# Chunked attention and mixture of experts: the first block's order from the list schedule

## The chip, the cores and the metric

The kernel runs on one NeuronCore of a Trainium2 chip. Five engines with queues of their own take part: TensorE (PE, its weight loads PEld), VectorE (DVE), ScalarE (ACT), GpSimd (POOL) and SyncE (SP), which issues the DMAs. The metric is the device time of one execution in microseconds; less is better.

## The reference

Attention in chunks of 32 queries, each chunk over 8 memory rows and a window of 16 + 32 + 8 keys, for 4 batches of 8 heads, 768 positions and 64 values a head. Its result, as 3072 tokens of 512 values, goes through 4 experts whose outputs are weighted and summed.

```python
def _attn_ref(q, k, v, mem_k, mem_v):
    for c in range(nc):                       # chunk 32, left 16, right 8
        k_full = np.concatenate([mem_k, k_ctx], axis=2)
        v_full = np.concatenate([mem_v, v_ctx], axis=2)
        scores = scale * np.matmul(q_c, k_full.transpose(0, 1, 3, 2))
        scores = scores - np.max(scores, axis=-1, keepdims=True)
        a = np.exp(scores)
        a = a / (np.sum(a, axis=-1, keepdims=True) + 1e-09)
        out[:, :, c_start:c_end] = np.matmul(a, v_full)

def _moe_ref(x, domain_probs, w1, w2):
    p = domain_probs / (domain_probs.sum(-1, keepdims=True) + 1e-09)
    for e in range(E):
        h = np.maximum(x @ w1[e], 0.0)
        out += p[:, e:e + 1] * (h @ w2[e])
```

## The kernel before

Attention works on units of 96 positions (three chunks) with all heads; there are 8 units a batch (u = 0 to 7) and 32 in all. Per unit: one load of queries and keys (`qk`), scores on TensorE (S, line 455), copies out of PSUM (line 476), maximum, subtraction, exponential, sum and reciprocal (lines 493 to 504), then products with the reciprocal into a banded matrix `band` (line 513), a transpose on TensorE (T, line 526) with copies into `aT` (line 532), and the product with `v` (X, line 540). X is split into a high and a low part, `xa_hi` and `xa_lo` for units 0 to 3, `xb_hi` and `xb_lo` for units 4 to 7 (lines 560, 566); their sum goes to `xr` (line 569).

Every fp32 product of the experts runs as three products of such parts. Weights are split too: a cast to the high part on ScalarE (line 594) and a subtraction for the low part on VectorE or GpSimd (line 598). A half of a batch is 384 tokens. For the first expert of the first batch, `w1` has 8 tiles f; one product for a tile and a half is 12 matmuls of up to 384 columns (line 640), followed by ReLU parts (lines 651, 652). The second product is 24 matmuls of 512 columns for each 128 tokens (line 684). Later batches use a scheme of seven products instead of eight (`Pair`, `Full`, `Halves`; lines 1112 and 1336).

The program has three parts. The first block covers all eight units of batch 0, the first product of half 0 and the second product of its 384 tokens. Its order on all engines is written out by hand in `FIRST_BLOCK`: Q and V are loads, r weight loads, h and lv, lp weight splits, W and w warm-up matmuls on zeros, S to xl the attention steps, M and N the first product on columns 0 to 191 and the rest (`HALVES` = 6: six of the eight tiles are cut so), g and G the halves of the second product. The second and third parts are plans: operations are added in TensorE's order with their engine, an estimated time, what they read and write, and a due time; `run` tries 60 list schedules with shifted due times and other engines, replays each against noise, keeps the best and emits the instructions in the order of its start times. TensorE's order in a plan is that in which the operations were added. The second part begins with the first product of half 1 (line 1047, `plain_first`), eight tiles f, and the third works on n from 5 to 15, with weights read back through a ring of nine tiles (`ring`). Every plan begins with all engines free at time 0 and all inputs there.

DMAs are in the plans as one queue on SP: an issue takes 0.1 us, the bytes pass at 330 GB/s, and nothing lands before 2.6 us:

```python
if op.engine == "SP":
    dma = max(dma, start + 0.3) + op.bytes / 330e3
    op.end = max(dma, start + 2.0) + 0.6
    free["SP"] = start + 0.1
```

Of the kernel before, what the change touches and what calls it, by code (L numbers as in the profile page):

```python
# [11 lines left out]
F32 = mybir.dt.float32  # L12
# [39 lines left out]
xl2 T3 m2 ev3 M5 m4 X3 m5 xh3 xl3 sh4 N0 p5 n0 h8 lp8 e4 N1 N2 h12 sh5 n1 h9 lp9 n2 e5 t4 h10 lv10 N3 n3 lv12  # L52
h11 N5 lp11 N4 n4 b4 n5 N6 h13 t5 b5 h14 N7 lp13 lv14 n6 h15 T4 ev4 n7 X4 xh4 T5 xl4 R0 lp15 ev5
V6 S6 S7 X5 xh5 p6 xl5 V7 sh6 g0 e6 p7 t6 b6 G0 sh7 e7 t7 b7 g1 T6 ev6 G1 T7 ev7 g2 X6 xh6 xl6 G2 X7 xh7 xl7
"""
HALVES = 6
# [4 lines left out]
SLACK = 25.0  # L61
ENGINES = ("PE", "ACT", "DVE", "POOL", "SP")

TURNS = 60
# [19 lines left out]
class Tile:  # L84


    def __init__(self, make, parts):
        self.make, self.parts, self._ap, self.ops = make, parts, None, []
        self.held = False

    @property
    def ap(self):
        if self._ap is None:
            self._ap = self.make()
        return self._ap


class Op:
    __slots__ = ("engine", "time", "fn", "deps", "succ", "birth", "due", "late", "ways", "early", "left", "ready", "start", "end",
                 "two", "bytes", "index")  # L100

    def __init__(self, engine, time, fn, birth, two, bytes_, index):
        self.engine, self.time, self.fn, self.birth, self.two, self.bytes = engine, time, fn, birth, two, bytes_
        self.deps, self.succ, self.index, self.ways = set(), [], index, None
        self.start = self.end = None


class Plan:
# [6 lines left out]
    def __init__(self):  # L115
        self.ops, self.writers, self.readers, self.tags, self.pe = [], {}, {}, {}, 0.0

    def tile(self, make, tag, bufs, parts=1):
        t = Tile(make, parts)
        places = self.tags.setdefault(tag, [])  # L120
        t.behind = None
# [6 lines left out]
    def have(self, ap, tag=None, parts=1):  # L128
        t = Tile(None, parts)
        t._ap, t.behind = ap, None  # L130
        if tag:
            self.tags.setdefault(tag, []).append(t)
        return t
# [9 lines left out]
    def add(self, engine, time, fn, reads=(), writes=(), two=False, bytes_=0, other=None):  # L143

        op = Op(engine, time, fn, self.pe, two, bytes_, len(self.ops))
        if other:
# [4 lines left out]
        for key in reads + writes:  # L151
            t = key[0] if isinstance(key, tuple) else key
# [17 lines left out]
    def run(self):  # L170

        ops = self.ops
# [6 lines left out]
        for op in ops:  # L179
            op.early = max([d.early + self.took(d) + self.wait(d, op) for d in op.deps], default=0.0)  # L180
            if op.engine == "PE":
# [1377 lines left out]
```

## Time and profile before

| | us |
|---|---|
| median of 3 runs | 1077.26 |
| lowest, highest | 1076.61, 1078.2 |
| the profiled execution | 1078.29 |
| its span, first to last instruction | 1076.5 |
| TensorE busy in the span | 1057.2 (98%) |
| VectorE, ScalarE, GpSimd busy | 754.2, 650.3, 339.2 |
| mean granted clock of TensorE | 0.992 |
| DMA, mean | 266 GB/s |

All stretches below are in microseconds from the start of the span. Busy times are those of one profiled execution. A granted clock of 1.00 is 2.4 GHz, 0.50 is 1.2 GHz. An idle time is put down to what released the instruction behind it.

### The profile page before, as it was taken

What the parts mean: (1) busy time and instruction counts of PE and PEld (TensorE: products, weight loads), DVE (VectorE), ACT (ScalarE), POOL (GpSimd) and SP (SyncE); (2) the same over time, 40 slices, a digit from 0 to 9 for tenths busy, and PEclk for the clock granted to TensorE, in tenths of its full rate; (3) what the DMA queues carried; (4) which work ended last, traced back from release to release, by engine and by line L of the source; (5) the groups of instructions that cost most, each with busy time, mean ns of one, the idle gap of its engine ahead of it and who ended that gap; (6) DMA issues with size and microseconds to landing.
All of it is one profiled execution on the core that took longest, in us unless ns stands there. A gap on an engine that the chain in (4) does not pass through costs nothing.

```text
span 1076.5 us, 20355 instructions
## 1 busy us (share of the span) xinstructions
PE 1057.2 (98%) x7412; PEld 1008.3 (94%) x7412; DVE 754.2 (70%) x1345; ACT 650.3 (60%) x1652; POOL 339.2 (32%) x326
## 2 busy tenths in 40 slices
PE   7989999999999999999999999999999999999998
PEld 6878898988989899999999999999999999999998
DVE  6866786857976347768798875857679564748474
ACT  6546885747855567585765866657593644435261
POOL 3523533636252124243242511215023211303030
PEclk8999999999999999999999999999999999999999
DMA  6535696977978579999998978878777977878783
GB/s 222 205 122 213 242 372 219 357 266 262 388 249 327 195 245 300 310 339 321 344 333 298 310 264 273 260 240 257 249 240 235 314 245 236 268 235 253 246 263 137
DMA packets 169364, 286.61 MB, mean 266 GB/s; under 512 B 14128, under 2 KB 108336, under 8 KB 169264
## 3 DMA queue, kind: packets, MB, share of 16 engines
q1 hardware_dynamic: 169264, 285.31, 77.9%
q8 instruction: 59, 0.97, 0.4%
q14 instruction: 41, 0.34, 0.1%
HBM read 216.06 MB, written 69.21 MB: 265 GB/s over the span
## 4 chain that ended last, share of the span: by engine, by line
PE 91%; DVE 5%; DMA 2%; ACT 1%; issue 1%; SPq 0%; DVEq 0%; ACTq 0%
PE a_ps L1112 23%; PE a_ps L1336 17%; PE moe_ps L1112 17%; PE moe_ps L1092 13%; PE moe_ps L1336 13%; PE s_ps L815 2%; DVE band L513 2%; PE x_ps L833 2%; PE moe_ps L1047 2%; PE moe_ps L640 1%; PE moe_ps L684 1%; DMA t<-s_t 1%; DMA ring<-t 1%; DMA qk_pair<-in_qk_dram 1%; PE x_ps L540 0%
## 5 line engine op out<-in xcount | busy, mean ns | idle before, releaser
L1092 PE MATMUL moe_ps<-w,h_hi 128*128 128x512 f32 x432 | 134.3, 392 | 0.0
L776 DVE TENSOR_TENSOR u<-moe_ps,u 128x384 f32<-128x384 f32 x120 | 66.5, 554 | 76.7 <-PE moe_ps L1112 55.5
L777 POOL TENSOR_TENSOR u<-u,u 128x384 f32<-128x384 f32 x38 | 48.6, 1278 | 179.9 <-DVE us L776 179.6
L765 ACT ACTIVATE u<-u 128x384 f32<-128x384 f32 x132 | 68.7, 524 | 57.8 <-DVE u L776 57.3
L763 ACT COPY u<-a_ps 128x384 f32<-128x384 f32 x120 | 57.1, 476 | 74.0 <-PE a_ps L1112 71.1
L1092 PEld LDWEIGHTS moe_ps<-w,h_hi 128*128 128x128 f32 x432 | 80.3, 188 | 16.9
L1092 PE MATMUL moe_ps<-w,h_lo 128*128 128x512 f32 x216 | 84.4, 391 | 0.0
L1066 DVE SCALAR_TENSOR_TENSOR acc<-a_ps,pr,acc 128x256 f32<-128x256 f32 x116 | 55.6, 480 | 40.0 <-PE a_ps L1336 39.0
L1336 PE MATMUL moe_ps<-ring,A_hi 128*128 128x256 f32 x440 | 81.9, 285 | 0.0
L776 DVE TENSOR_TENSOR A_lo<-u,A_hi 128x384 fp32r<-128x384 f32 x108 | 68.3, 639 | 16.7 <-ACT A_hi L763 16.7
L1066 DVE SCALAR_TENSOR_TENSOR acc<-moe_ps,pr,acc 128x256 f32<-128x256 f32 (+1 forms) x109 | 56.5, 523 | 32.0 <-PE moe_ps L1336 20.0
L887 DVE STREAM_TRANSPOSE aT<-band 32x256 f32<-32x256 f32 x168 | 73.0, 435 | 5.1 <-ACT band L763 2.1
L1112 PE MATMUL a_ps<-xc_hi,ring 128*128 128x384 f32 x352 | 75.5, 336 | 0.0
L1336 PEld LDWEIGHTS moe_ps<-ring,A_hi 128*128 128x128 f32 x440 | 69.9, 194 | 0.0
L1336 PE MATMUL a_ps<-ring,Sa_hi 128*128 128x256 f32 x352 | 65.8, 286 | 2.3 <-DMA ring<-t 2.3
L763 ACT CAST A_hi<-u 128x384 fp32r<-128x384 f32 x132 | 67.1, 512 | 1.0
L869 ACT ACTIVATE s_sb<-s_sb,mx 96x64 f32<-96x64 f32 x192 | 64.4, 337 | 0.7
L777 POOL TENSOR_TENSOR A_lo<-u,A_hi 128x384 fp32r<-128x384 f32 x24 | 25.9, 1083 | 123.4 <-ACT A_hi L763 77.7
L1336 PE MATMUL a_ps<-ring,A_hi 128*128 128x256 f32 x352 | 64.7, 283 | 0.1
L1336 PE MATMUL a_ps<-ring,Sb_hi 128*128 128x256 f32 x352 | 64.8, 283 | 0.0
L1336 PE MATMUL moe_ps<-ring,A_lo 128*128 128x256 f32 x220 | 62.7, 285 | 0.0
L1112 PEld LDWEIGHTS a_ps<-xc_hi,ring 128*128 128x128 f32 x352 | 61.8, 188 | 0.1
(217 smaller groups left out, 3081.7 us busy)
## 6 DMA issues: line engine op xcount, KB each, us to landing
ring<-k SPq DMA_DIRECT2D x132, 512.0 KB, 4.8
ring<-t SPq DMA_DIRECT2D x88, 512.0 KB, 5.5
ring<-w SPq DMA_DIRECT2D x66, 512.0 KB, 5.4
k<-w SPq DMA_DIRECT2D x48, 512.0 KB, 5.2
w<-w SPq DMA_DIRECT2D x40, 512.0 KB, 5.8
raw<-in_w_dram SPq DMA_DIRECT2D x64, 256.0 KB, 5.0
ring<-k SPq DMA_DIRECT2D x44, 256.0 KB, 4.4
qk_t<-in_qk_dram SPq DMA_DIRECT2D x24, 448.0 KB, 5.4
```

The source lines that it names most:

```text
L513: eng.tensor_tensor(out=band[rows, :, at:at + hi - lo], in0=s[rows, :, lo:hi], in1=sm[rows].broadcast_to([CH, H, hi - lo]), op=ALU.mult,)
L763: nc.scalar.copy(out(), x())
L765: nc.scalar.activation(out(), x(), func)
L776: ("DVE", t_dve(cols), lambda: nc.vector.tensor_tensor(out=out(), in0=x(), in1=y(), op=op)),
L777: ("POOL", t_pool(cols), lambda: nc.gpsimd.tensor_tensor(out=out(), in0=x(), in1=y(), op=op)),
L815: nc.tensor.matmul(s_ps.ap[0:UQ, j * NPAIR + g, :], lhsT=qk_t.ap[rows, g * UQ:(g + 1) * UQ], rhs=qk_t.ap[rows, NPAIR * UQ + g * P:NPAIR * ...
L869: now["plan"].add("ACT", t_act(KW) + 0.01, lambda h=h: nc.scalar.activation(s_sb.ap[:, h, :], s_sb.ap[:, h, :], AF.Exp, bias=mx.ap[:, h, : ...
L887: dve(lambda c=c, kb=kb: nc.vector.transpose(out=aT[kb * CH:(kb + 1) * CH, :, c * CH:(c + 1) * CH], in_=band[c * CH:(c + 1) * CH, :, kb * ...
L1066: dve(lambda: nc.vector.scalar_tensor_tensor(out=o.ap[:, cols], in0=ps_ap(), scalar=p_e, in1=o.ap[:, cols], op0=ALU.mult, op1=ALU.add), n_ ...
L1092: nc.tensor.matmul(self.ps.ap, lhsT=h.ap[:, self.rows], rhs=w.ap[:, part, :], start=(i == 0 and k == 0), stop=(i == NF - 1 and k == 2),)
L1112: nc.tensor.matmul(ps.ap[:, 0:SG], lhsT=a()[:, c * P:(c + 1) * P], rhs=y[:, k0 + c, :], start=(first and i == 0), stop=(i == len(steps) - ...
L1336: nc.tensor.matmul(ps.ap[:, cols], lhsT=x.ap[:, rows], rhs=w_ap[:, y, :], start=(begins and k == 0 and i == 0), stop=(k == NP2 - 1 and i = ...
```

## The change

The first block's hand-written order for all engines goes. `FIRST_BLOCK` now names TensorE's operations alone, in an order of its own, and a plan of its own adds all operations of the block and is searched with 600 tries. W is a group of matmuls on zeros (into spare columns of the bank of X). The order of the units on TensorE is T0, T1, T3, T2, T5, T4, T7, T6. Four of the eight tiles are cut in two (`AHEAD`), at 192 columns; the others run on all 384 at once. Units in `STRAIGHT` multiply into the band as before, on VectorE or GpSimd as the plan chooses; the others (0, 3, 5) multiply in place and copy into the band on ScalarE. Copies out of PSUM may go to ScalarE or VectorE. All units from 2 on have score tiles of their own, the 16 weight tiles share eight places, and `xc` lies where these tiles were.

The estimate of a DMA changes in all plans (the first plan keeps 330 GB/s). Each plan takes over from the one before when the engines become free and when its values are there. The plans are tried 100 times instead of 60, and scored by when TensorE is done, the last one by its end.

```diff
+FIRST_TURNS, FIRST_SEED = 600, 1
 FIRST_BLOCK = """
-Q0 r1 r0 r2 Q1 Q2 Q3 r3 r4 Q4 Q5 r5 r7 V0 W40 V1 r6 P0 h0 S0 lv0 h1 p0 S1 lv1 h2 p1 h3 sh0 lv2 S2 sh1 e0 lp3
-p2 S3 e1 p3 t0 S4 b0 T0 h4 t1 b1 lp4 Sa5 ev0 X0 p4 T1 sh2 xh0 ev1 e2 Sb5 X1 xl0 V2 h5 r11 t2 w8 xh1 xl1 h7 b2
-lp5 V3 h6 lp6 Q6 Q7 r9 r8 lp7 r12 r10 r13 r14 V4 r15 sh3 V5 M0 m0 M1 m1 T2 ev2 M2 M3 e3 t3 X2 b3 M4 xh2 m3
...
+W32 S0 S1 S2 W6 S3 W30 T0 W6 X0 T1 W12 X1 S4 W12 M1 T3 M5 X3 M2 T2 S5 X2 S6 M6 N7 N5 N4 N6 N0 N2 T5 N1 N3 S7 X5
+g0 T4 g1 G0 X4 T7 G1 X7 T6 g2 X6 G2
 """
-HALVES = 6
+AHEAD = (0, 2, 2, 0, 0, 2, 2, 0)
+STRAIGHT = (1, 2, 4, 6, 7)
+ASIDE = (6,)
+DMA_ISSUE, DMA_FIRST, DMA_RATE = 0.45, 2.0, 400e3
-TURNS = 60
+TURNS = 100
...
             if e == "SP":
-                dma = max(dma, start + 0.3) + op.bytes / 330e3
-                end[op.index] = max(dma, start + 2.0) + rng.uniform(0.4, 1.4)
-                free[e] = start + 0.1
-        return max(end)
+                dma = max(dma, start + DMA_FIRST) + op.bytes / self.rate
+                end[op.index] = dma + rng.uniform(0.2, 0.9)
+                free[e] = start + DMA_ISSUE
+            op.end = end[op.index]
+        self.done = free
+        return max(end) if self.last else free["PE"]
...
-                dma = max(dma, start + 0.3) + op.bytes / 330e3
-                op.end = max(dma, start + 2.0) + 0.6
-                free["SP"] = start + 0.1
+                dma = max(dma, start + DMA_FIRST) + op.bytes / self.rate
+                op.end = dma + 0.5
+                free["SP"] = start + DMA_ISSUE
...
     def took(self, op):
-        return max(2.6, 2.0 + op.bytes / 330e3) if op.engine == "SP" else op.time
+        return DMA_FIRST + op.bytes / self.rate + 0.5 if op.engine == "SP" else op.time
...
+    def after(self, keys=()):
+        zero = self.done["PE"]
+        free = {e: max(-4.0 if e == "SP" else 0.0, t - zero) for e, t in self.done.items()}
+        ends = {}
+        for key in keys:
+            ends[key] = max([0.0] + [op.end - zero + LATENCY for op in self.writers.get(key, ())])
+        return free, ends
...
-    now = {"plan": Plan()}
+    now = {"plan": Plan({"PE": 0.9, "SP": 0.6, "ACT": 2.0, "DVE": 0.8, "POOL": 4.6}, rate=330e3)}
...
+    spots = fixed(early, "spot", 8)
+    raw_spots = fixed(raw, "raw", 3) + acc_tiles[:3] + spots[:2]
+    s_spots = [t[0:UQ].rearrange("p (h k) -> p h k", h=H) for t in spots[2:]]
+    def zeros(n):
+        def fn():
+            for _ in range(n):
+                nc.tensor.matmul(x_bank[:, DM - P:DM], lhsT=idle, rhs=idle, start=True, stop=True)
+        pe(0.111 * n, fn, [], [])
...
+        if u not in STRAIGHT:
+            dve(lambda: nc.vector.tensor_tensor(
+                out=s.ap, in0=s.ap, in1=sm.ap.broadcast_to([UQ, H, KW]), op=ALU.mult), n_s, [sm], [s], two=True)
...
+                if u in STRAIGHT:
+                    join(dst, src, lambda rows=rows, n=hi - lo: sm.ap[rows].broadcast_to([CH, H, n]), ALU.mult, cols,
+                         [(s, c), sm], [("band", u % 2, c, at)])
+                else:
+                    act(dst, src, cols, [(s, c)], [("band", u % 2, c, at)])
...
+    for word in FIRST_BLOCK.split():
+        now["plan"].word = word
+        do_word(word.rstrip("0123456789"), int(word.lstrip("WSTXMNgG")))
+    with tc.manual_schedule():
+        now["plan"].run(FIRST_TURNS, FIRST_SEED)
...
+    free, ends = before.after(keys)
+    plan = now["plan"] = Plan(free)
```

## Rows read from the trace of the kernel before

**Rows 1.** TensorE's waits from 26.5 us on: engine, line, releaser, total, times, longest

```profile
PE att_ps L526 <- DVE band L513: 3.8, 4, 1.8
PE moe_ps L640 <- ACT xa_hi L560: 0.6, 1, 0.6
PE moe_ps L1047 <- ACT xb_hi L560: 0.6, 1, 0.6
PE x_ps L540 <- ACT aT L532: 0.6, 1, 0.6
...
PE a_ps L1336 <- DMA ring<-t: 2.3, 1, 2.3
```

**Rows 2.** Busy time by stretch, all engines; last granted clock, DMA share, GB/s

```profile
core 0: us, PE busy (x) PEld busy (x) DVE busy (x) ACT busy (x) POOL busy (x), PEclk, DMA share, GB/s
0.00:84.00 84.00, 70.92 (x609) 61.74 (x610) 56.83 (x96) 45.27 (x98) 33.71 (x39) 0.92 0.52 176
...
30.00:60.00 30.00, 27.19 (x273) 25.52 (x274) 26.68 (x49) 16.08 (x40) 16.90 (x14) 1.00 0.58 210
...
500.00:550.00 50.00, 50.00 (x382) 48.86 (x383) 39.29 (x77) 38.13 (x105) 16.46 (x17) 1.00 0.99 338
```

**Rows 3.** TensorE by stretch: length, busy, granted clock, DMA share, GB/s

```profile
13.00:15.00 2.00, 0.28 (x4) 1.00 1.02 360
16.00:26.00 10.00, 8.06 (x64) 0.52 0.50 121
72.00:74.00 2.00, 0.55 (x7) 1.00 0.00 0
74.00:78.00 4.00, 4.00 (x14) 0.57 0.38 115
```

**Rows 4.** TensorE's timeline in the first block: start, duration, line, operation

```profile
1.00 4.45 PE L409 MATMUL moe_ps<-idle 128*128 128x128 bf16 x40 [1.00 <-POOL idle L398]
26.79 1.12 PE L640 MATMUL moe_ps<-xa_hi,w 128*128 128x192 f32 x8
30.39 0.85 PE L526 MATMUL att_ps<-ident,band 96*128 96x96 f32 x8 [0.69 <-DVE band L513]
31.02 1.12 PE L640 MATMUL moe_ps<-xa_hi,w 128*128 128x192 f32 x8
...
68.02 0.83 PE L526 MATMUL att_ps<-ident,band 96*128 96x96 f32 x8
```

**Rows 5.** The chain that ended last, first block: start, duration, what

```profile
40.65 8.30 PE moe_ps L640 x72
56.92 2.07 PE att_ps L455 x32
74.30 4.37 PE moe_ps L684 x12
79.48 2.98 PE moe_ps L684 x12
82.46 0.84 PE x_ps L540 x16
83.85 10.86 PE moe_ps L1047 x60
```

**Rows 6.** Timeline of ScalarE and VectorE, unit 6, and a later unit's band copies

```profile
60.22 1.81 ACT L476 COPY s_sb<-att_ps 32x512 f32<-32x512 f32 x4
62.06 0.68 DVE L493 TENSOR_REDUCE mx<-s_sb 96x8 f32<-96x512 f32 x1 [1.14 <-ACT s_sb L476]
62.78 0.69 DVE L494 TENSOR_TENSOR s_sb<-s_sb,mx 96x512 f32<-96x512 f32 x1
64.29 0.68 DVE L502 TENSOR_REDUCE sm<-s_sb 96x8 f32<-96x512 f32 x1 [0.83 <-ACT s_sb L498]
65.44 2.30 DVE L513 TENSOR_TENSOR band<-s_sb,sm 32x64 f32<-32x64 f32 x3
105.17 1.99 ACT L763 COPY band<-s_sb 32x64 f32<-32x64 f32 x4
```

**Rows 7.** The page's DMA issues: count, size of one, median us to landing

```profile
ring<-t SPq DMA_DIRECT2D x88, 512.0 KB, 5.5
```

More of the change, by code (lines that the diff above doesn't have):

```diff
@@ L126, in tile, with slot, have @@
         return t
-    def have(self, ap, tag=None, parts=1):
+    def slot(self, tag, aps, parts=1):
+        t = self.tile(None, tag, len(aps), parts)
+        t._ap = t.behind._ap if t.behind else aps[len(self.tags[tag]) - 1]
+        return t
+    def have(self, ap, tag=None, parts=1, ends=()):
         t = Tile(None, parts)
-        t._ap, t.behind = ap, None
+        t._ap = ap
         if tag:
             self.tags.setdefault(tag, []).append(t)
+        self.ends.update(((t, i), end) for i, end in enumerate(ends))
         return t
@@ L251, in replay @@
             e = op.engine
-            start = free[e]
+            start = max(free[e], op.floor)
             for d in op.deps:
@@ L398, in tile_chunked_attention_moe @@
     nc.gpsimd.memset(idle, 0.0)
-    spare = {}
-    def warm(n, late=False):
-        if late not in spare:
-            if late:
-                spare[late] = ps_head.tile([P, H, P], F32, name="att_ps")[:, 0, :]
-            else:
-                spare[late] = ps_moe.tile([P, DM], F32, name="moe_ps")[:, 0:P]
-        for _ in range(n):
-            nc.tensor.matmul(spare[late], lhsT=idle, rhs=idle, start=True, stop=True)
     ident = head.tile([P, P], F32, name="ident")
@@ L772, in dve, with moved @@
         now["plan"].add("DVE", t_dve(cols), fn, reads, writes, two)
+    def moved(out, x, cols, reads, writes):
+        now["plan"].add("ACT", t_act(cols, True), lambda: nc.scalar.copy(out(), x()), reads, writes,
+                        other=("DVE", t_dve(cols), lambda: nc.vector.tensor_copy(out=out(), in_=x())))
     def join(out, x, y, op, cols, reads, writes, eng="DVE", psum=False):
@@ L1383, in combine_some, with fixed @@
             make2_combined(*combined.pop(0))
-    plan = now["plan"]
-    w1_of = {}
-    for which, f in made:
-        t = plan.have(None, "w1" if which == 1 else "w2", 4 if which == 1 else 2)
+    def fixed(pool, name, many):
+        return [pool.tile([P, DM], F32, name=name, bufs=many) for _ in range(many)]
+    spots = fixed(early, "spot", 8)
+    acc_tiles = fixed(opool, "acc", 6)
+    raw_spots = fixed(raw, "raw", 3) + acc_tiles[:3] + spots[:2]
+    s_spots = [t[0:UQ].rearrange("p (h k) -> p h k", h=H) for t in spots[2:]]
@@ new lines, in tile_chunked_attention_moe, with early_weights @@
+    x_bank = ps_x.tile([P, DM], F32, name="x_ps")
+    x_out = x_bank[:, 0:NPAIR * UQ].rearrange("p (g q) -> p g q", g=NPAIR)
+    first = {}
+    def zeros(n):
[3 more added lines that the diff above has]
+        pe(0.111 * n, fn, [], [])
+    def early_weights(which, f):
+        r = now["plan"].slot("raw_spot", raw_spots)
+        dma(lambda: r.ap, lambda: (w1 if which == 1 else w2)[0, f], P * DM * 4, [], [r])
@@ new lines, in band_keys, with early_turn, fn @@
+    def band_keys(u):
+        return [("band", u % 2, c, at) for c in range(NCU) for _, _, at in PIECES[c]]
+    def early_turn(u):
+        early_band(u)
+        half = H // 2
+        if u in ASIDE:
+            banks = [bank() for _ in range(2)]
+            a_ps = [lambda t=t: t.ap.rearrange("p (h q) -> p h q", h=half) for t in banks]
+        else:
+            t_ps = new(lambda: ps_head, [P, H, P], "att_ps", 2, parts=2)
+            banks = [(t_ps, i) for i in range(2)]
+            a_ps = [lambda i=i: t_ps.ap[:, i * half:(i + 1) * half, :] for i in range(2)]
+        for i in range(2):
+            def fn(i=i):
+                for h in range(half):
+                    nc.tensor.transpose(a_ps[i]()[:, h, 0:UQ], bands[u % 2][:, i * half + h, :], ident[0:UQ, 0:UQ])
+            pe(0.35, fn, band_keys(u), [banks[i]])
+        for i in range(2):
+            moved(lambda i=i: aTs[u % 2][:, i * half:(i + 1) * half, :], lambda i=i: a_ps[i]()[:, :, 0:UQ],
+                  half * UQ, [banks[i]], [("aT", u % 2, i)])
@@ L1514, in tile_chunked_attention_moe @@
     with tc.manual_schedule():
-        plan.run()
+        plan.run(last=True)
 _INS = ["qk", "v", "probs", "w1", "w2"]
```

468 lines of the change are left out of this document (188 added, 280 removed).

## The prediction

> **What bounds the kernel now.** I read TensorE's waits first, on both sides of 84 us. Behind that point a single wait of any size is left, 2.3 us for a `ring` load in nearly a millisecond; ahead of it stand those for VectorE's `band` products, 3.8 us, and three of 0.6 [rows 1]. The table by stretches says the same: of the first 84 us TensorE is busy for 70.9, so 13.1 us are idle [rows 2]. The whole matter is therefore the first block. Its end is the start of the first matmul of line 1047, at 83.85 us [rows 5], which stood 0.6 us behind `xb_hi` [rows 1].
>
> Idle time isn't all that is lost there. Between 16 and 26 us the granted clock is 0.52, between 74 and 78 it is 0.57: the engine ran mostly at 1.2 GHz instead of 2.4. Ahead of the first drop it had been busy for 0.28 of 2 us (13 to 15), ahead of the second for 0.55 of 2 (72 to 74) [rows 3]. And VectorE is busy for 26.7 of the 30 us from 30 to 60, ScalarE for 16.1 and GpSimd for 16.9 [rows 2]. So the block is a chain per unit, from the scores S over the softmax to the transpose T and the mix X, through a nearly full VectorE; TensorE waits at the T's.
>
> **TensorE's line behind the first M.** Prices at 2.4 GHz: 12 matmuls of 192 columns 1.38 (8.30 for 72), two S 2.07, 12 matmuls of the second product 2.98, X 0.84, 12 matmuls of 384 columns 2.17 (10.86 for 60) [rows 5]; T 0.63, from its start to the next operation's [rows 4]. Before, behind M0 at 26.79 [rows 4]: twelve halves 16.6, two full products 4.3, six T 3.8, six X 5.0, S6 and S7 2.1, 72 matmuls of the second product 17.9. That is 49.7 of the 57.1 us to 83.85. The other 7.4 are 5.6 us of waits (3.8 and three times 0.6 [rows 1]), 1.4 us of low clock (the 12 matmuls from 74.30 took 4.37 instead of 2.98 [rows 5]) and a rest of 0.4.
>
> In the new order only four of the eight products are cut in two (`AHEAD`): eight halves 11.1, four full ones 8.7. With T 3.8, X 5.0, S5 to S7 3.1 and the second product's 17.9, TensorE has 49.6 us of work behind M1. The recut wins 1.1 us, and S5, now behind M1, takes 1.0 back.
>
> **The front, up to M1.** SP now takes up the `qk` loads by their due times, and the three weight loads that stood between the first and the second have late ones; so units 1 to 3 come sooner, which costs nothing. S0 followed the 40 warm-up matmuls, which end at 5.45 [rows 4]; W32 ends at 4.6, and the load had landed by 5.45 at the latest. I take 5.0, so S0 ends at 6.0. A straight unit, unit 6, which had VectorE to itself, took 7.8 us from its first copy out of PSUM (60.22) to its transpose (68.02) [rows 4, 6]. Unit 0 is not straight: it puts one product (as the subtraction, 0.69) and four ScalarE copies (1.99) in the place of three VectorE products in a row (2.30) [rows 6], 0.4 longer: T0 at 14.3.
>
> VectorE then sets T1. Per unit it gives 0.68 (maximum), 0.69, 0.68 (sum), 0.47 up to the band (65.44 less the sum's end) and 2.30 for a straight one, so 4.8; or 0.69 in place of 2.30, so 3.2 [rows 6]. From 7.9 (S0's end, and four copies 1.81) it has units 0 and 1 done at 15.9, and with some 2 us of waiting for the exponentials T1 comes at 17.9.
>
> The warm-up words W are now in TensorE's order and cost time where nothing else holds it: 0.111 us each (4.45 for 40 [rows 4]). W6, S3 and W30 end at about 13.1, under T0's wait. T1 ends at 18.5, W12 at 19.9, partly over the copies that X1 needs. X1 and S4 end at 21.8. The product behind X7 could start 1.39 us behind X7's start [rows 5], so M1 could run at 21.8; the last W12 hides behind nothing and costs 1.3. M1 at 23.1, 3.7 us before M0.
>
> **Stalls behind M1.** Down the line T3 is due at 24.5 and T2 at 28.7. VectorE, free of unit 1 at 17.9, has two `x_lo` (1.0 by estimate, from 0.69 for 512 columns) and unit 3 (3.2), ScalarE the copies (2.0): 24.1. Unit 2, straight, is done at 26.9, but low parts of weights and `h_lo` come in between. Nothing to 3 us are lost here. I take 1.5, since one wait of 0.69 stood ahead of T2 before [rows 4]. The four later T's have their S 11 us or more ahead, and need 1.04 + 7.8; the N products and the second product hide them. Over units 0, 3 and 5 VectorE gets rid of 4.8 us, GpSimd of three products, and ScalarE, the least busy [rows 2], gets 6 more. That PSUM copies may go to VectorE moves work by the planner's choice; ScalarE's four take 1.81 now [rows 6], so it can win up to 0.9 in a chain or lose as much on VectorE, and I count nothing.
>
> Without gaps as those ahead of the two drops I expect no low clock behind M1. The block ends at 23.1 + 49.6 + 0.4 + 1.5 = 74.6; 9.25 us are won.
>
> **The other parts.** The 16 weight tiles now share eight places: a load on SP can stand behind the split of the tile before it, and everything queued on SP behind it stands too, `v` loads among it. Their bound is zero to 1 us; I take zero, since no product of line 640 waited for a weight before, only for `xa_hi` [rows 1]. `xc` lies where the early tiles were and is written by the next plan only; that plan's first eight products (8 x 2.17 = 17 us) use neither `xc` nor new weights, and hide its wait and the first loads. If that cover went, each us would count. The times handed from plan to plan, and 100 tries for 60, rearrange the side engines of 990 us in which TensorE hardly waits: at best the 2.3 us go, at worst waits of that size come. I take 0.
>
> The DMA estimate goes from 0.1 to 0.45 us an issue, for a lone load of 512 KB from 3.6 to 3.8 us in the due times and 2.6 to 3.8 in the schedule (median to landing 5.5 [rows 7]), and from 330 to 400 GB/s. The last one leaves the rows: with 0.99 of DMA time taken, 338 GB/s were moved [rows 2]. Nine loads in a row are 11.8 us at 400 and 14.0 at 338, so the last is expected 2.2 us early. The Trainium skill speaks against the new rate too: "DMA: Bandwidth & Descriptors", section Specifications, gives about 358 GB/s as HBM's limit for one core. By that figure the nine loads take 13.2 us, 1.4 more than planned; the row lies still lower and agrees.
>
> **The sum.** The profiled execution took 1078.29 us, 1.79 more than its span of 1076.5; the median of the runs, 1077.26, lies 0.76 above that span. 1077.26 - 9.25 = 1068.0 us.
>
> **Rivals.** A: VectorE stays the bound. For it speak its 26.7 of 30 us and the tight T3 and T2, against it the 4.8 us that it loses. Then the stretch behind M1 loses its 7.4 us again, the block ends at 23.1 + 49.6 + 7.4 = 80.1, and 3.75 us are won: 1073.5. B: the plan fits. No stall behind M1 (1.5), the last W12 stands in a real wait (1.3), and the wait for the ring load goes (2.3): 1068.0 - 5.1 = 1062.9. For it speaks that the order leaves TensorE no other hole behind M1; against it, that the side engines have some 10% of air at best. C, the other side: ring loads come late. One wait of 2.3 us came in the third plan, which has 11 rounds (n from 5 to 15). If the rate of 400 lets each round's T loads go out that much too late, ten more cost 23 us: 1091. From five on it decides (5 x 2.3 = 11.5 > 9.25). For it speaks the 2.2 us just worked out; against it, that a lone load is now given more time, which pulls issues ahead. D: the change doesn't do what it says. The new search and the handed times lose outside the block what it wins, say four waits of 2.3: 1077.
>
> **How the numbers follow.** Forecast 0.55, A 0.18, B 0.14, C 0.08, D 0.05. From 1061.5 to 1074 the range holds the forecast, nearly all of B, and A; it leaves out C and D. About 0.2%, 2.2 us, is what a measurement of this kernel can tell from no change. Faster by more are the forecast, A and B: 0.87. Same is D: 0.05. Slower is C: 0.08.
>
> **What would show it.** T0 near 14.3, the first M near 23.1, the first matmul of the other half near 74.6; a granted clock of 1.0 from the first M on; no more than some 3 us of TensorE waits behind the block. Rival A shows in waits for `band` of 4 us or more behind M1, C in several waits for `ring`. I am wrong if the block ends behind 80 us or if more than 5 us of waits stand behind it.

## The result and the profile after

The changed kernel takes 1079.21 us (median of 22 runs, 1076.39 to 1083.63), the kernel before beside it 1076.83 (22 runs): a ratio of 1.0021, 95% interval 1.0011 to 1.0031. 1068 was predicted. The profiled execution took 1079.78 us, its span is 1078.0.

The first block came out as worked out. Busy time by stretch of the changed kernel, to be read against [rows 2]:

```profile
core 0: us, PE busy (x) PEld busy (x) DVE busy (x) ACT busy (x) POOL busy (x), PEclk, DMA share, GB/s
0.00:84.00 84.00, 75.81 (x691) 68.01 (x692) 59.24 (x108) 49.05 (x104) 28.90 (x37) 1.00 0.62 213
30.00:60.00 30.00, 29.53 (x248) 27.26 (x247) 27.65 (x54) 20.13 (x44) 10.29 (x10) 1.00 0.59 211
500.00:550.00 50.00, 48.43 (x353) 46.91 (x349) 37.58 (x70) 36.73 (x102) 15.76 (x17) 1.00 0.95 321
```

From 30 to 60 us TensorE is idle for 0.5 us instead of 2.8; VectorE is as full as before (27.65 of 30), and the granted clock is 1.00 throughout. TensorE's timeline has T0 at 15.41, the first product M1 at 23.02 and the first product of the other half, now line 794, at 74.23, where [rows 5] have it at 83.85:

```profile
15.41 0.85 PE L1249 MATMUL att_ps<-ident,band 96*128 96x96 f32 x8 [2.49 <-issue]
...
23.02 1.11 PE L794 MATMUL moe_ps<-xa_hi,w 128*128 128x192 f32 x8
24.98 0.88 PE L1249 MATMUL att_ps<-ident,band 96*128 96x96 f32 x8 [0.35 <-ACT band L503]
...
74.23 1.55 PE L794 MATMUL moe_ps<-xb_hi,w 128*128 128x384 f32 x8
```

So 9.62 us are won by then, and none of them is left at the end. The third row above says where to look: from 500 to 550 us TensorE was never idle before, now it is for 1.6 us. Its waits behind 26.5 us, against [rows 1] (line 860 is the first, line 1084 the second product of the later batches; lines 503 and 521 are the helpers that record ScalarE's copies and VectorE's sums):

```profile
PE a_ps L860 <- ACT u L503: 3.9, 4, 1.4
PE a_ps L860 <- DVE u L521: 3.0, 3, 1.5
PE a_ps L1084 <- DVE A_lo L521: 0.8, 1, 0.8
PE x_ps L1268 <- DVE aT L517: 0.6, 1, 0.6
PE x_ps L1268 <- issue: 0.5, 1, 0.5
PE a_ps L1084 <- DVE acc L814: 0.2, 1, 0.2
```

The wait for `ring` is gone, and 7.9 us of waits for copies and sums have come: 7.1 us for those that free TensorE's banks in PSUM (the copies and sums `u` and `acc`), 0.8 for an operand (`A_lo`).

**The account.** From the first product of line 794 (1047) on, TensorE runs the same 6804 matmuls in the same order in both kernels, so each start can be set against its own start before. Where the difference grows from one matmul to the next by over 0.15 us, I call that an added gap. It counts from start to start, so it is a little longer than the idle time of the same wait (1.59 us for one of 1.43). In these two traces, in us:

| | |
|---|---|
| first block | -9.62 |
| added gaps in the second plan (120 to 396 us of before's time) | +2.56 |
| added gaps in the third plan (396 to 626) | +8.55 |
| waits that only the kernel before has (2.48 at the ring load, 0.34 and 0.26) | -3.07 |
| small differences, under 0.15 us each | +3.13 |
| the last matmul | +1.55 |

In the small ones lies another 1.4 us from 606 to 626: in the kernel before the granted clock fell behind that wait for the ring load, as these windows of its trace show.

```profile
core 0: us, PE busy (x), PEclk, DMA share, GB/s
618.00:620.00 2.00, 0.00 (x0) 1.00 0.96 319
620.00:622.00 2.00, 1.89 (x11) 0.66 1.06 386
622.00:624.00 2.00, 2.00 (x11) 0.50 0.79 274
624.00:626.00 2.00, 2.00 (x19) 0.98 0.37 84
```

Without it the small differences add up to 4.5 us on the other side, spread over the whole run. Two things are to be found, then: who makes the gaps, and what makes the matmuls themselves slower.

### The profile page after: what moved, and what is told of

It is laid out like the page before. It is cut to its first block, busy times and chain, and to the rows that moved or that the text cites. A ratio compares the mean times of both kernels' runs of the same rounds, so it can differ in the third digit from the quotient of the medians.

```text
span 1078.0 us, 20402 instructions
## 1 busy us (share of the span) xinstructions
PE 1057.8 (98%) x7438; PEld 1006.6 (93%) x7438; DVE 747.2 (69%) x1319; ACT 649.1 (60%) x1652; POOL 365.0 (34%) x351
## 4 chain that ended last, share of the span: by engine, by line
PE 83%; DMA 7%; DVE 4%; ACT 3%; POOL 2%; issue 1%; SPq 0%; POOLq 0%; ACTq 0%; DVEq 0%
PE a_ps L860 19%; PE a_ps L1084 16%; PE moe_ps L860 14%; PE moe_ps L840 12%; PE moe_ps L1084 12%; PE moe_ps L794 3%; DMA t<-s_t 2%; PE s_ps L560 2%; DMA t<-t_hi 2%; DMA raw<-in_w_dram 2%; PE x_ps L579 2%; POOL s_t L522 2%; ACT s_sb L615 1%; DVE s_t L521 1%; DMA raw_pair<-in_w_dram 1%
## 5 line engine op out<-in xcount | busy, mean ns | idle before, releaser
L840 PE MATMUL moe_ps<-w,h_hi 128*128 128x512 f32 x480 | 149.6, 393 | 0.0
L840 PEld LDWEIGHTS moe_ps<-w,h_hi 128*128 128x128 f32 x480 | 88.9, 188 | 18.7
L840 PE MATMUL moe_ps<-w,h_lo 128*128 128x512 f32 x240 | 93.8, 391 | 0.0
L521 DVE TENSOR_TENSOR A_lo<-u,A_hi 128x384 fp32r<-128x384 f32 x108 | 74.4, 693 | 19.6 <-ACT A_hi L503 19.4
L522 POOL TENSOR_TENSOR u<-u,u 128x384 f32<-128x384 f32 x33 | 40.1, 1214 | 102.6 <-DVE us L521 98.2
L522 POOL TENSOR_TENSOR u<-u,us 128x384 f32<-128x384 f32 x40 | 46.7, 1168 | 52.9 <-DVE us L521 40.2
```

The costliest lines, as they stand in the source:

```text
L521: ("DVE", t_dve(cols), lambda: nc.vector.tensor_tensor(out=out(), in0=x(), in1=y(), op=op)),
L522: ("POOL", t_pool(cols), lambda: nc.gpsimd.tensor_tensor(out=out(), in0=x(), in1=y(), op=op)),
L840: nc.tensor.matmul(self.ps.ap, lhsT=h.ap[:, self.rows], rhs=w.ap[:, part, :], start=(i == 0 and k == 0), stop=(i == NF - 1 and k == 2),)
```

## The experiments

Theories on the gaps. E: the new estimate of DMAs makes worse second and third plans. G: the other engines and the DMAs can't follow a TensorE that comes earlier, whatever the plan. L: each search is a draw, and this one was unlucky. H, that the handed-over times do it, needs no run: without them the search gives both plans the same order on every engine. On the slower matmuls, P: the place of the tiles.

What all runs gave, ahead of their story. The times are medians, block and gaps come from one profiled execution of each kernel. "330" and "400" are the rate in the estimate of the plan, "old" its form before (0.1 us an issue, nothing before 2.6 us), "new" its form after (0.45 us, 2.0 us ahead of the bytes). Block: start of the other half against before's profiled 83.85. Gaps: added gaps as above, in us.

| kernel | plan 2 | plan 3 | block | gaps, plan 2 | gaps, plan 3 | median | ratio to before |
|---|---|---|---|---|---|---|---|
| before_seed2 | old 330 | old 330 | 0.1 | 0.2 | 1.3 | 1075.07 | 0.9980 |
| before_seed3 | old 330 | old 330 | -1.1 | 0.5 | 1.9 | 1074.93 | 0.9977 |
| before_newdma | new 400 | new 400 | -0.6 | 0.3 | 8.1 | 1083.71 | 1.0056 |
| before_xc_far | old 330 | old 330 | -1.6 | 0 | 0 | 1080.45 | 1.0024 |
| changed kernel | new 400 | new 400 | -9.6 | 2.6 | 8.6 | 1079.21 | 1.0021 |
| seed2 | new 400 | new 400 | -7.9 | 1.1 | 3.8 | 1073.91 | 0.9969 |
| seed3 | new 400 | new 400 | -7.3 | 0.8 | 5.7 | 1076.50 | 0.9993 |
| tries500 | new 400 | new 400 | -7.8 | 0 | 5.6 | 1076.19 | 0.9995 |
| x_near | new 400 | new 400 | -9.6 | 0.6 | 8.4 | 1075.81 | 0.9989 |
| first3 | new 400 | old 400 | -8.4 | 0.7 | 8.6 | 1079.41 | 1.0016 |
| other | old 330 | new 400 | -8.3 | 6.0 | 7.8 | 1083.85 | 1.0075 |
| all_old | old 330 | old 330 | -7.1 | 5.0 | 0.8 | 1079.81 | 1.0021 |
| old_dma | old 330 | old 330 | -9.9 | 4.6 | 0.2 | 1075.48 | 0.9983 |
| old_dma_late | old 330 | old 330 | -7.8 | 3.1 | 0 | 1081.66 | 1.0038 |
| rate23_near | new 330 | new 330 | -7.0 | 7.0 | 1.6 | 1077.57 | 1.0006 |
| mix | new 400 | old 330 | -7.9 | 1.0 | 0 | 1070.55 | 0.9934 |
| rate3 | new 400 | new 330 | -8.3 | 0.6 | 1.6 | 1071.52 | 0.9940 |
| mix_near | new 400 | old 330 | -9.6 | 0.4 | 0.2 | 1068.13 | 0.9909 |
| mix_near_seed2 | new 400 | old 330 | -8.4 | 0 | 1.3 | 1068.27 | 0.9917 |

Several kernels share a plan, operation for operation. The changed kernel's second plan is also that of x_near, first3, mix, rate3 and mix_near, and its gaps there are 0.4 to 2.6 us: on one and the same order they differ by 2 us, and the changed kernel's profile has the most. x_near and other have its third plan too, rate23_near has rate3's. all_old's third plan is that of before; mix, mix_near and old_dma_late have old_dma's.

The wait of 2.3 us for the ring load stands in the profiles of three kernels only, before, before_xc_far and all_old; in the others it is gone, which counts 2.5 us and the low clock behind it for them.

### Undoing the plans' new rules: all_old and old_dma

all_old keeps the new block and gives the second and third plan all their old rules (`self.old` is true for these two plans):

```diff
-TURNS = 100
+TURNS = 60
...
-                dma = max(dma, start + DMA_FIRST) + op.bytes / self.rate
-                end[op.index] = dma + rng.uniform(0.2, 0.9)
-                free[e] = start + DMA_ISSUE
+                if self.old:
+                    dma = max(dma, start + 0.3) + op.bytes / 330e3
+                    end[op.index] = max(dma, start + 2.0) + rng.uniform(0.4, 1.4)
+                    free[e] = start + 0.1
...
-        return max(end) if self.last else free["PE"]
+        return free["PE"] if self.rate == 330e3 else max(end)
...
-    plan = now["plan"] = Plan(free)
+    ends = dict.fromkeys(ends, 0.0)
+    plan = now["plan"] = Plan()
```

> The new first block stays; the two later plans are made by the old rules (DMA estimate of 0.1 us an issue, 330 GB/s, landing from 2.6 us; 60 tries; score by the last end; no times handed over). Theory E (the new DMA estimate makes worse plans behind the block): TensorE's waits behind the block are those of before, some 3 us, and the 9.6 us won in the block stay: about 1067 to 1068 us. Theory G (the side engines or the DMAs can't follow a TensorE that is 9.6 us early, so it is given back whatever the plan): 1076 to 1079, with 8 us or more of waits behind the block. Theory L (each new search is a draw; the one of before was a good one): anything from 1068 to 1079.

old_dma undoes the estimate alone (the second group of these lines, in `schedule` and `took` too) and keeps the tries, the score and the handed times.

> The changed kernel with the old DMA estimate in the two later plans, and nothing else undone (100 tries, new score). Theory E: as with all the old rules, 1067 to 1069 us. If the number of tries or the score is what hurts: 1077 to 1080. Theory G: 1076 to 1079. Theory L: anything from 1068 to 1079.

They took 1079.81 us (ratio 1.0006 to 1.0037) and 1075.48 (0.9966 to 0.9999). Both have next to no gaps in the third plan, and both have 4.6 to 5.0 us in the second, where the changed kernel has 2.6. The gain is given back in either case, but in another place: E as it stood then, 1067 to 1069 us, missed both.

### The estimate alone behind the old block: before_newdma

```diff
...
-                dma = max(dma, start + 0.3) + op.bytes / 330e3
-                op.end = max(dma, start + 2.0) + 0.6
-                free["SP"] = start + 0.1
+                dma = max(dma, start + 2.0) + op.bytes / 400e3
+                op.end = dma + 0.5
+                free["SP"] = start + 0.45
...
```

> The kernel before, hand-written first block and all, with the new DMA estimate in its two plans and nothing else. Theory E: the waits of the changed kernel behind the block come without its block: some 8 to 11 us more than before, 1085 to 1088 us. Theory G: nothing to give back, so 1076 to 1079. Theory L: anything from 1076 to 1088.

1083.71 us, ratio 1.004 to 1.0072, 1.3 us under E's range and clear of G's. The gaps of the third plan are here too, 8.1 us at the same places (the largest at 455 and 482 us), though TensorE comes 9 us later than in the changed kernel. For the third plan that is E, and against G. Its order is close to the changed kernel's (some nine tenths of the operations stand in the same sequence), so the two are hardly two draws.

### Other draws: seed2, seed3, tries500, before_seed2, before_seed3

seed3 and before_seed3 have 3 for 2.

```diff
-    def run(self, turns=TURNS, seed=1, last=False):
+    def run(self, turns=TURNS, seed=2, last=False):
```

> The changed kernel with another seed (2 instead of 1) for the search of the two later plans; the first block is the same. Theory E: the estimate is wrong in every draw, so 1076 to 1081 us. Theory L: a different time, anywhere from 1068 to 1082, with waits in other places. Theory G: 1076 to 1079.

> The changed kernel with seed 3 in the later plans (1 gave 1079.2 us, 2 gave 1073.9). Theory L: a third value between 1068 and 1082. Theory G: 1074 to 1079, since no draw keeps much of the 9.6 us.

```diff
-TURNS = 100
+TURNS = 500
```

> The changed kernel with 500 tries for each later plan instead of 100, seed 1 as in the change. Theory L: a longer search finds a plan with fewer waits behind the block; waits there 3 to 5 us instead of 8, and 1069 to 1074. Theory E (the estimate itself misleads the search): no better than with 100 tries, 1077 to 1081. Theory G: 1076 to 1079.

```diff
-        rng = random.Random(1)
+        rng = random.Random(2)
```

> The kernel before with seed 2 instead of 1 in the searches of its two plans; block, estimate and tries are its own. Theory L (each search is a draw, and the one of before a good one): slower than before by some us, 1079 to 1086, with waits behind the block where before has 3 us. The plans' own scores by their model are 305.5 and 695.1 us for this seed, 306.1 and 691.4 for that of before: from them 3 us slower. Theory G (an early TensorE is held back whatever the plan): nothing is early here, so 1076 to 1078.

> The same with seed 3; its plans score 306.0 and 693.3 us by their own model, 1.8 more than those of before. Theory L: 1077 to 1085, another time than with seed 2. Theory G: 1076 to 1078.

1073.91, 1076.50 and 1076.19 us for the changed kernel, 1075.07 and 1074.93 for the one before. So a draw is worth 2 to 5 us, and the change's was a poor one (L has a share); that before's was a good one, as L had it, is not so, since both others lose the wait for the ring load. But all draws by the new estimate have 3.8 to 8.6 us of gaps in the third plan, and no draw by the old one has over 1.9. Five times as many tries gave 3.0 us, no more than another seed does (2.7 and 5.3), and left 5.6 us of gaps there.

### Splitting the estimate by plan: mix and other

```diff
     def __init__(self, free=None, ends=None, rate=DMA_RATE):
         ...
+        self.old = False
...
     plan = now["plan"] = Plan(*plan.after(
         ...
     ))
+    plan.old = True
```

> The changed kernel with the old estimate of a DMA in the third plan alone; the first and the second plan keep the new one. Theory E, now split by plan: the traces so far give TensorE's added gaps from 445 to 626 us of before's time (third plan) as 0.2 to 2.5 us in the kernels planned by the old estimate and 3.8 to 8.5 us in those planned by the new one, whichever first block stands ahead; in the second plan (120 to 300 us) it is the other way round behind the new block, 4.6 to 5.0 us by the old estimate and 0 to 2.6 us by the new. By E this kernel keeps the better half of each: gaps of at most 2.6 us in the second plan and at most 1.5 us in the third, so about 1069 us (ratio near 0.993). By L (each search is a draw, the estimate means nothing) the gaps add to 5 to 11 us as in the others, 1074 to 1080 us. By G (what follows cannot keep up with an early TensorE) the block's gain is gone by 626 us whatever the estimate: 1075 us or more.

other sets `plan.old` for the second plan instead.

> The changed kernel with the old estimate of a DMA in the second plan alone, the mirror of mix. E by plan: added gaps of TensorE of 4 to 5 us from 120 to 300 us of before's time (all_old 5.0, old_dma 4.6) and of 4 to 8.5 us from 445 to 626 us, so 1079 us (old_dma's 1075.5 plus 4 to 8 us in the third plan) to 1083 us. If the second plan's share was chance, it has under 2.6 us of gaps there and the time is that of the changed kernel or less, 1076 to 1079 us.

1070.55 us (ratio 0.9918 to 0.9949) and 1083.85 (1.0048 to 1.0102): E to 1.6 us in mix, and just beyond the upper end of E in other. The two kernels do the same work and differ by 13 us through its order and place on the side engines alone. It is not that TensorE comes early, either: at 445 us of before's time it is 1.4 us ahead of before in other, which has 7.8 us of gaps in the third plan, 6 us ahead in mix, which has none, and 8.9 ahead in mix_near (below), which has 0.2. That ends G for the third plan. All that TensorE waits for in mix behind 75 us is

```profile
PE a_ps L873 <- ACT u L516: 0.4, 1, 0.4
```

Side by side, the stretch of the third plan in the changed kernel and, 8 us earlier, in mix:

```profile
445.00:485.00 40.00, 36.70 (x238) 34.82 (x237) 29.40 (x49) 28.62 (x74) 17.43 (x17) 1.00 0.98 341
```

```profile
437.00:477.00 40.00, 40.00 (x277) 39.49 (x276) 26.61 (x50) 28.75 (x83) 13.75 (x15) 1.00 0.97 326
```

The DMAs are just as full, and loads of 512 KB take as long (medians for `ring<-k` 6.0 us from 440 to 610 us, and 5.9 from 432 to 602 in mix); TensorE is idle for 3.3 us in the one and never in the other. Nothing is faster in mix, it is only queued otherwise. The gap at 451.54 in the changed kernel shows how. Its timeline, TensorE, ScalarE, VectorE and GpSimd:

```profile
451.54 0.96 PE L860 MATMUL a_ps<-xc_hi,ring 128*128 128x384 f32 x4 [1.43 <-ACT u L503]
```

```profile
450.05 0.52 ACT L505 ACTIVATE u<-u 128x384 f32<-128x384 f32 x1 [2.34 <-DVE u L521]
450.60 0.51 ACT L503 CAST A_hi<-u 128x384 fp32r<-128x384 f32 x1
451.02 0.47 ACT L503 COPY u<-a_ps 128x384 f32<-128x384 f32 x1
```

```profile
444.26 1.21 DVE L521 TENSOR_TENSOR s_t<-s_t,t_hi 128x512 fp32r<-128x512 f32 x1 [1.86 <-POOL s_t L522]
...
447.19 2.23 DVE L633 STREAM_TRANSPOSE aT<-band 32x256 f32<-32x256 f32 x5
449.45 0.56 DVE L521 TENSOR_TENSOR u<-moe_ps,u 128x384 f32<-128x384 f32 x1
```

```profile
441.51 1.09 POOL L522 TENSOR_TENSOR s_t<-raw 128x256 f32<-128x256 f32 x1 [10.12 <-DVE acc L814]
...
444.18 0.74 POOL L522 TENSOR_TENSOR s_t<-raw 128x256 f32<-128x256 f32 x1
```

TensorE waits for a bank. The product that the copy at 451.02 takes out of it was ready by 449.1 at the latest, but the copy stands on ScalarE behind two operations on `u`; these wait 2.34 us for VectorE's sum (449.45), which stands behind 2.2 us of transposes that TensorE needs only at 469 us; and VectorE had lost 1.86 us waiting for GpSimd's part of `s_t`, which GpSimd began after 10.12 us of idle time that, by the trace, a sum of VectorE's ended. The DMAs' part is the same in both kernels: GpSimd's `s_t` sums wait for the store `t<-s_t` to give their buffer free, 18.9 us from 445 to 490 us here and 19.6 in mix's stretch. No DMA ends a wait of TensorE; each link is an in-order queue with something late ahead of something urgent. That the rate makes these gaps is tried below; how it leads the search to such an order is read from this one gap, and not shown further.

### Rate or form: rate3, first3 and rate23_near

```diff
-    ))
+    ), rate=330e3)
```

> The changed kernel with the rate of a DMA in the third plan's estimate at 330 GB/s in place of 400; its form (0.45 us of issue, 2.0 us to the first byte, queueing) stays new. The stretch moved 285 to 341 GB/s at a share of 0.87 to 0.98. If the rate is what misleads the planner, the gaps from 445 to 626 us fall from 8.5 us to under 2.5 us and the time to about 1071 us, as in mix. If it is the form, the gaps stay at 4 to 9 us and the time at 1075 to 1080 us.

first3 is mix with 400e3 for 330e3 in the old form.

> Mix with 400 GB/s in place of 330 in the old estimate of the third plan; its form (0.1 us of issue, nothing on the ring of transfers before 0.3 us, at least 2.0 us to land, 0.4 to 1.4 us of scatter) stays old. If the rate is what misleads the planner, the gaps from 445 to 626 us rise to 4 to 9 us and the time to 1075 to 1079 us; if it is the form, they stay under 2.5 us and the time at mix's 1070 to 1071 us.

1071.52 us (0.9922 to 0.9958) and 1079.41 (1.0002 to 1.0029), with 1.6 and 8.6 us of gaps in the third plan: there it is the rate, and the form has no part that shows. Over all runs that makes six different orders of the third plan at 400 GB/s, with 3.8 to 8.6 us of gaps, and six at 330, with 0 to 1.9. The waits of TensorE in first3 are of the changed kernel's kind again:

```profile
PE a_ps L873 <- ACT u L516: 5.9, 5, 2.1
PE a_ps L873 <- DVE u L534: 1.0, 1, 1.0
```

rate23_near has 330 GB/s in the new form in both plans, and the place of x_near (below).

```diff
-    plan = now["plan"] = Plan(free)
+    plan = now["plan"] = Plan(free, rate=330e3)
```

> Mix_near's place of the tiles, with the new form of the estimate and a rate of 330 GB/s in both the second and the third plan. In the third plan rate3 had 1.3 us of gaps by it, so at most 2.5 us here. In the second plan, if the rate is what counts there too (330 GB/s makes it worse behind the new block), the gaps from 120 to 300 us are 4 to 5 us and the time about 1071 to 1072 us; if the form is (the new form makes it better), they stay under 2.6 us and the time is that of mix_near, 1067 to 1069 us.

1077.57 us (0.9992 to 1.002), 6 us more than the worse of the two expectations for it: 7.0 us of gaps in the second plan, 5.1 of them one wait for a cast of weights on ScalarE, which stood behind GpSimd's sums:

```profile
PE a_ps L861 <- ACT w L504: 5.0, 1, 5.0
```

So the third plan wants 330 GB/s. For the second plan behind the new block the runs point to 400, but less firmly: four orders at 400 have 0 to 2.6 us of gaps there, three at 330 (all_old's, old_dma's, which other and old_dma_late share, and this one) 3.1 to 7.0. All three come from seed 1 and the first two are nearly alike; another seed at 330 was not run, and behind the old block three orders at 330 have at most 0.5. So it is not told apart from the draw. Rows of windows with the DMAs full fit both rates: in the second plan (rate23_near)

```profile
140.00:160.00 20.00, 20.00 (x119) 17.11 (x118) 14.93 (x31) 17.46 (x57) 7.64 (x8) 1.00 1.02 388
200.00:220.00 20.00, 20.00 (x112) 19.25 (x111) 16.24 (x27) 12.00 (x27) 13.38 (x13) 1.00 1.04 406
```

they move 388 to 406 GB/s, in the third (mix)

```profile
512.00:552.00 40.00, 40.00 (x288) 38.82 (x287) 34.58 (x64) 33.22 (x83) 16.30 (x16) 1.00 1.03 343
```

343, as 338 in [rows 2]. The packets differ: from 120 to 215 us in the kernel before, and from 432 to 602 in mix,

```profile
DMA packets 11905, 29.30 MB, mean 308 GB/s; under 512 B 1242, under 2 KB 2522, under 8 KB 11896
```

```profile
DMA packets 33932, 55.40 MB, mean 326 GB/s; under 512 B 2235, under 2 KB 21714, under 8 KB 33913
```

21% of them are under 2 KB in the second plan's stretch, 64% in the third's. That a plan does best with the rate that its own stretch moves fits all runs behind the new block, with the doubt just stated for the second; that the small packets set that rate is argued from these rows and was not tried apart.

### TensorE later: old_dma_late

48 products more behind the block, whose sums nothing reads.

```diff
         now["plan"].run(FIRST_TURNS, FIRST_SEED)
+        for _ in range(48):
+            nc.tensor.matmul(x_bank[:, 0:SG], lhsT=xa[0][:, 0, 0:P], rhs=xa[0][:, 0, :], start=True, stop=True)
```

> The kernel old_dma (new block, second and third plan by the old estimate of a DMA) with 48 products of 128x384 more behind the block, whose sums nothing reads, so that TensorE enters the second plan some 8.3 us later (48 at 173 ns) while the other engines and the transfers go on. The second plan is the same. Old_dma's trace has gaps of 1.3, 1.9 and 1.0 us at 138 and 188 us of before's time, and the kernels with the old block and that estimate have none there. G: the gaps come because TensorE is early against transfers and casts, which cannot be moved; with TensorE 8.3 us later they vanish, and the whole is only 3 to 4 us longer than old_dma, 1079 us. If the order of the side engines is what holds TensorE (L or E), the gaps stay and the whole is 8 us longer, 1083 to 1084 us.

1081.66 us (1.0026 to 1.0051), 6.2 more than old_dma, between the two expectations. The 48 run behind the first eight matmuls of the other half, from 77.43 us on. TensorE enters the second plan 10.4 us later than in old_dma's profile and has 3.1 us of gaps there instead of 4.6; 2.6 us go at four places, 1.1 come at two others. So G may have a share in the second plan, 1.5 us of 4.6 by the gaps and 2.1 by the medians (6.2 longer for 8.3 us of products), but the same order gives gaps that differ by as much; most of them stay with the order.

### The place of the tiles: before_xc_far and x_near

```diff
+    xcp = ctx.enter_context(tc.tile_pool(name="xcp", bufs=1, side="right"))
...
-        for name, n in (("xa", NC), ("xb", NC), ("xc", 6))
+        for name, n in (("xa", NC), ("xb", NC))
     )
+    xc = tuple(xcp.tile([P, 6, SG], F32R, name=f"xc_{part}") for part in ("hi", "lo"))
```

> The kernel before with nothing altered but the place of the tiles xc_hi and xc_lo: at the far end of SBUF, where the changed kernel has them, so that all behind xb_lo lies 18,432 bytes a partition lower, as it does there; every engine's order of instructions stays. Theory P: in the six kernels with the new first block the products of xa and xb with ring slots take 338 to 339 ns by the profile's rows against 336 ns in the four with the old block (behind 640 us), the same in all six to 0.01 us by stretches of 100 us, which no difference of plans can do; the place of the tiles is what the six share. By P those rows read 338 to 339 ns here, the stretch from 626 us to the end grows by 1.7 us and the whole by about 3 us, 1080 us against 1077. If the place is not the reason, the rows stay at 336 ns and the time at that of before, within 0.1%.

```diff
+    xp = ctx.enter_context(tc.tile_pool(name="xp", bufs=1, side="right"))
...
-    xa, xb = (in_parts(const, name, NC) for name in ("xa", "xb"))
+    xa, xb = (in_parts(xp, name, NC) for name in ("xa", "xb"))
```

> The changed kernel with xa and xb moved to the far end of SBUF as well, beside xc, as they are neighbours in the kernel before; every engine's order of instructions stays. By P in its narrow form (the products of xa and xb suffer where xc lies far from them) they come back from 339 to 336 ns and the time falls by about 3 us, to 1076 us. If what slows them is not the distance from xc, they stay at 339 ns or get slower, and the time stays at 1079 us or rises.

1080.45 us (1.0009 to 1.0039) and 1075.81 (0.9973 to 1.0006), against 1078.10 and 1079.21: P, in both directions. Groups of instructions from 640 to 1060 us (line, operands, shapes, count, busy us, mean ns): before, before_xc_far, x_near.

```profile
L1112 PE MATMUL moe_ps<-xa_hi,ring 128*128 128x384 f32 x112 | 24.0, 336 | 0.0
```

```profile
L1114 PE MATMUL moe_ps<-xa_hi,ring 128*128 128x384 f32 x112 | 24.3, 339 | 0.0
L1114 PE MATMUL moe_ps<-xc_hi,ring 128*128 128x384 f32 x112 | 23.9, 334 | 0.0
```

```profile
L861 PE MATMUL moe_ps<-xa_hi,ring 128*128 128x384 f32 x112 | 24.0, 335 | 0.0
L861 PE MATMUL moe_ps<-xc_hi,ring 128*128 128x384 f32 x112 | 23.9, 334 | 0.0
```

Three nanoseconds on each product of xa and xb, and before_xc_far's small differences add up to 3.7 us from the block's end to the last matmul, with no gap at all. With xa and xb beside xc, at the far end, they are gone. From 626 us to the end, where no plan has gaps, the small differences are 1.69 us in before_xc_far and in the changed kernel alike, and 0.04 in x_near. Not all that x_near wins is the place, though: of the 4.1 us by which its profiled execution is ahead of the changed kernel's at the last matmul, 2.0 are small differences and 1.9 are gaps of the second plan, on the same order. In the changed kernel it is every second product, in the groups of xa and xb behind products of xc, which takes 179 ns from start to start instead of 173. Which relation of addresses does it stays open.

### Both together: mix_near and mix_near_seed2

> Mix (third plan by the old estimate of a DMA) with xa and xb moved to the far end beside xc, as in x_near. If the two causes, the plans and the place of the tiles, are separate, their gains add: mix is at 1070.55 us, its products of xa and xb at 339 ns come to 335 to 336 ns and give back the 3.7 us that the place cost in before_xc_far, so 1067 us (ratio 0.990). If moving the tiles disturbs the plans by other ways (buffers that come free later), it stays near 1070 us.

> Mix_near with seed 2 of the random search in the second and third plan. E (the estimate decides, the seed only scatters): TensorE's added gaps from 445 to 626 us of before's time stay under 2.5 us, as in the five kernels whose third plan goes by the old estimate, and under 2.6 us from 120 to 300 us; the time is 1066 to 1071 us. L (mix was a lucky draw): gaps of 4 to 9 us in the third plan again, 1072 to 1077 us.

1068.13 us (ratio 0.9892 to 0.9925) and 1068.27 (0.9891 to 0.9943). mix_near comes within 1.1 us of the 1067 expected if the gains add, and a second draw gives the same time: mix was not luck. This version beats both kernels. All that TensorE still waits for in mix_near behind 74 us, 990 us long, is

```profile
PE a_ps L874 <- ACT u L517: 0.2, 1, 0.2
```

## Why the prediction was wrong

**The block: right.** T0 came at 15.41 (14.3), M1 at 23.02 (23.1), the other half at 74.23 (74.6). Behind M1 the T's waited for the band by 0.35 us where 1.5 were taken, but two X's waited for 0.6 and 0.5, so that the sum of the stalls, 1.5, came true at other places than named. 9.62 us against 9.25. In the mean of the 15 profiled executions with this block it is 8.3, since the clock falls for a while ahead of M1 in eleven of them (last section); by them the term was some 1 us too large.

**"I take 0" for the later plans: the step that failed.** The working reads "The times handed from plan to plan, and 100 tries for 60, rearrange the side engines of 990 us in which TensorE hardly waits ... I take 0", and the paragraph on the estimate ends without a price. In its place the profile has 11.1 us of gaps (2.56 and 8.55); the 8.55 come back in every kernel with this third plan (7.8 to 8.6), of the 2.56 some 2 us were this one execution's. The reason behind the zero, that TensorE hardly waited there, was read the wrong way round: that row told of the old plan, which the edit threw away. What it should have been read for is how thin the cover was: with DMAs at 0.99 of their time, a plan that takes them for nearly a fifth faster than they are (400 against 338 GB/s) puts casts, sums and copies in a worse order on three in-order queues. Of the edits named in that sentence, the handed times do nothing, and neither 60 tries (before_newdma, 8.1 us of gaps in the third plan) nor 500 (5.6) change the picture.

**The rate: seen, and priced in the wrong place.** The text did find that 400 GB/s leaves the rows, since [rows 2] have 338 at a share of 0.99, and gave it to rival C as late ring loads, one wait of 2.3 us a round. The cause was right, for the third plan, and the way was not: the changed kernel has no wait for `ring` at all, its waits are for PSUM copies behind late sums. So C did not come, and its 1091 was too much. For the second plan the argument was not borne out: 400 was the better rate in the orders that were run. The Trainium skill's figure of about 358 GB/s as HBM's limit for one core ("DMA: Bandwidth & Descriptors", Specifications, which divides a stack's 716 by two cores) was cited against 400 GB/s; the third plan's 343 lies below it, the second plan's windows of 20 us at 388 and 406 above it, and there the measurement decides.

**Rival D came nearest.** It has the new search lose outside the block what the block wins, 1077 us at a chance of 0.05. It was thought of as accident, four waits of 2.3 us; it is a cause that acts in all six orders of the third plan at 400 GB/s.

**The place of `xc`: not costed as a place.** "`xc` lies where the early tiles were" was looked at for waits alone, and rightly found free of them. That its address would slow the products of two other tiles, 3.7 us in all, no row of before could have told.

**What was left out on the other side.** The wait for the ring load went, as rival B had it for 2.3 us, and gave 4.1 with the low clock behind it (2.48 + 1.6 in mix_near). It goes in before_seed2 and before_seed3 too and stays in all_old, so it hangs on the third plan's order and not on the block. That the kernel without the two losses lands at 1068.13, next to the 1068.0 predicted, is in part luck: the block is a little smaller, this gain was not in the sum, and small losses that the medians do not resolve make up the rest.

## What to carry over

Where a list schedule makes the order, its cost table is part of the kernel: an edit to an estimate rewrites every queue behind it, and idle time in the old profile says nothing on the new order. Set a transfer's rate by the stretch that the plan covers, from windows in which the DMAs are full: one rate for all cost the third plan some 8 us here. And when a program's matmuls run in one order in two versions, set start against start: it splits a lost gain into gaps and slower instructions in one pass.

## What the runs showed of the hardware

**The place of an operand changes a matmul's time.** Same instructions, same order, other addresses of the moving operand's tiles: 336 against 339 ns by the rows above, 3.7 us a run.

**The same first block finds the clock in two ways.** TensorE is idle for 2.5 us ahead of T0 in each of the 15 executions of the new block. From 16 to 30 us the granted clock then is 1.00 in four and 0.78 to 0.89 in eleven of them, a fall to 1.2 GHz for a part of that stretch. The changed kernel's and seed2's windows:

```profile
16.00:30.00 14.00, 11.71 (x145) 10.18 (x143) 12.93 (x23) 11.81 (x27) 4.46 (x5) 1.00 0.63 227
```

```profile
16.00:30.00 14.00, 11.93 (x128) 10.52 (x128) 12.07 (x22) 10.90 (x25) 5.12 (x5) 0.88 0.69 226
```

and, of TensorE alone, seed2 again:

```profile
core 0: us, PE busy (x), PEclk, DMA share, GB/s
18.00:20.00 2.00, 2.00 (x19) 0.50 0.80 246
```

The four won 9.6 to 9.9 us by the block's end, the eleven 7.0 to 8.4; from 26 us on the clock is 1.00 in all of them. T0's start, 15.2 to 16.3, has a share in that too. The 15 are executions of different programs that have this block in common; but the changed kernel's own 22 runs, too, have a mean granted clock of 1.00 in two and of 0.995 to 0.998 in twenty. So some 2 us of the block are decided anew from execution to execution, and the changed kernel's profile is one of the rarer kind.

**DMAs that are full move 388 to 406 GB/s in one stretch and 343 in another** at the same busy share, and the transfers of 256 to 512 KB in mix's stretch of the third plan take 4.7 to 6.7 us from issue to landing (medians by tile), where a plan counts 3 to 4 for a lone one.
